# Windowed attention with block summaries and a two-layer MLP in one kernel: new loading order at the start, a private tile for the picking matrix, whole-tile copies at the end, and a newly planned order of all work

## The chip, the cores and the metric

The kernel runs on one core of a Trainium2 chip. The metric is the device time of one execution in microseconds (us), smaller is better. Five engines work side by side, each in its own fixed order: PE (TensorE, matrix products), DVE (VectorE), ACT (ScalarE), POOL (GpSimd) and SP (SyncE, which here issues nearly all DMA transfers). They wait for one another by semaphores.

## The reference, cut to what matters

```python
def _attn_ref(q, k, v):                       # 4 batches, 8 heads, 768 positions, 64 per head
    k_sum = k.reshape(B, H, nb, 32, D).max(axis=3)       # 24 block summaries of the keys
    v_sum = v.reshape(B, H, nb, 32, D).mean(axis=3)      # and of the values
    mask_l = np.abs(pos[:, None] - pos[None, :]) < 16    # near keys only
    ...
    a = softmax(concat([near scores, scores against k_sum + log(32)]))
    return a @ concat([v, v_sum])

def _moe_ref(x, w_in, w_out):                 # x: 3072 x 512 from the attention
    h = x @ w_in                              # 512 -> 2048
    g = h * erf(softplus(h))
    return g @ w_out                          # 2048 -> 512
```

## The kernel before

**Tiling.** The 3072 rows are 6 chunks of 512. A chunk's attention is 4 *quads* (`qd`), each two heads by 512 queries. A block of 64 queries multiplies a window of 96 keys (`LW`) and the 24 summaries (`NS`), 120 columns (`NK`) in all. Quads 0 to 3 of the first batch are special: their keys are cut out of the plain transposed keys (`kfirst`, tiles `kf`) instead of a prepared window array. The first block has 16 keys of zero padding ahead of it, and `near` in `scores` multiplies the first 16 real keys in their stead, for the mask hides those columns. The summaries of the first batch's values come from PE: `vsum_first` multiplies the values (`vt`) by a 0/1 matrix `pick`, in six matmuls to one bank, `vs`. ACT copies the result to `vsum`, and `rows_` spreads it under the value windows `vwf`, which `load_vw_first` had filled with 128 partitions, zeros at the bottom.

**A quad's path.** `scores` (PE, L597), maxima, exponentials and norm (DVE L636, ACT L644, DVE L654; from quad 4 on a fused DVE operation at L630), `transp` (PE L684 and copies to the tile `pt` at L689; from quad 8 on DVE and a trip through DRAM, `dt` out and `ptd` back), `av` (PE L729 or L732, output `px`), `xsplit` (x as a high and a low part, the low one at DVE L748).

**MLP.** The weights come as raw 64-bit numbers (`rw`, L334, 1024 KB a unit). `convert` makes 32-bit floats of them on DVE (L354, L357, L360), and `split` a high part (ACT) and a low part (DVE L376), both in `w`. `mm1` (PE L836) takes three products of the high and low parts, and from period 8 on `products` (L879 to L888) takes fewer products of sums. `mm2` is L1006 (two periods) and L1010, three products of the split tiles `gh` and `gl`; `gl` is made at DVE L993. A period is 512 rows by 512 hidden columns, 24 in all.

**Order.** The code adds each piece of work to a `Plan` with booked times per engine, and `Plan.order` plays the engines against each other and hands out an order for each one. `TUNE` shifts single pieces by number: an offset of the sorting key, a price for changing ACT's function table, which table, and an engine. Where a piece may run on two engines, `order` picks one. At the start `busy` fills expected waits of PE with matmuls on zeros (tile `idle`, L1058). `first_dma` books the first transfers.

**End.** `evac_last` empties the last four banks. For the tiles 0 to 2, ACT copies one half and DVE the other, each to a tile of its own and with a transfer of its own; tile 3 is copied whole by ACT and sent in two halves, from ACT's and SP's queues.

Of the kernel before, what the change touches and what calls it, by code (L numbers as in the profile page):

```python
# [11 lines left out]
F32 = mybir.dt.float32  # L12
# [10 lines left out]
C, F = 512, 2048  # L23
# [168 lines left out]
def block_attention_mlp(ctx: ExitStack, tc: tile.TileContext, q_t, k_nat, k_win, v_tok, v_nat, v_win, w_in, w_out, out):  # L192
# [91 lines left out]

# [9 lines left out]
    def first_dma(us, fn, r=(), w=(), **kw):  # L294
        return P.add({"SP": us}, lambda e: fn(), r, w, hold=2.0, land=-1.0, **kw)
# [216 lines left out]

    def load_v_first():
        for n in range(2):
            first_dma(2.1 + 0.15 * n, lambda n=n: nc.sync.dma_start(out=vts[n], in_=v_tok[3 * n:3 * n + 3].rearrange("t s c -> s t c")), w=[f"vt{n}"])  # L515

    def load_vw_first(p):
        first_dma(1.35, lambda: nc.sync.dma_start(out=st[p]["vw"], in_=v_win[0, p]), w=[f"vwf{p}"])

    def ksum_first(p):  # L520
        on({"DVE": 0.86}, lambda e: e.tensor_reduce(ksum[:, 0, p], groups(kfirst[p]), op=ALU.max, axis=AX.X), [f"kf{p}"], [f"ksum0{p}"])

    def vsum_first(bank):
        def go(t):
            if t == 0:
                tiles[bank] = ps("vs", bank)
            nc.tensor.matmul(tiles[bank][0:NK], lhsT=pick[:, 20 - 4 * t:140 - 4 * t], rhs=vts[t // 3][:, t % 3], start=(t == 0), stop=(t == 5))
        for t in range(6):
            pe(0.87, lambda t=t: go(t), [f"vt{t // 3}"], [bank])
        def summed():  # L530
            nc.scalar.copy(vsum[LW:NK], tiles[bank][LW:NK].rearrange("s (p c) -> s p c", p=NP))
        act(0.5, summed, [bank], [f"vsum0{p}" for p in range(NP)])
        def rows_(e, p):
            o, i = st[p]["vw"][LW:NK], vsum[LW:NK, p:p + 1, :].to_broadcast([NS, NB, 128])
            e.dma_start(out=o, in_=i) if e is nc.sync else copy(e, o, i)
        for p in range(NP):
            on({"ACT": 0.95, "SP": 0.45} if p else {"DVE": 1.13, "ACT": 0.95}, lambda e, p=p: rows_(e, p), [f"vsum0{p}", f"vwf{p}"], [f"vwg{p}"])
# [36 lines left out]

    PA = ("pA", "pB")

    def scores(qd, banks=PA):
# [29 lines left out]
        if qd >= NP:  # L607
            pe(0.98 if qd >= MQ else 1.56, both, [f"qb{qd % 2}", f"kw{qd % 2}"] + (["mh"] if qd < MQ else []), banks, small=1)
        else:
            pe(0.58, mask, ["mh"], banks, small=1)  # L610
            pe(0.96, lambda: keys(near), [f"qf{qd}", f"kf{qd}"], banks, small=1)
            pe(0.5, lambda: keys(lambda r, j: [(LW, ksum[r, 0, qd])]), [f"qf{qd}", f"ksum0{qd}"], banks, small=1)
# [104 lines left out]
    def av(qd, bank):  # L717
# [3 lines left out]
        def go():  # L721
            xo = s["xo"] = ps("px", bank)
            for j in range(NB):
                o = slice(64 * j, 64 * j + 64)
                for a in range(2):
                    r = slice(64 * a, 64 * a + 64)
                    if qd < DT:
                        b = 64 * (NI * a + j // 2)
                        nc.tensor.matmul(xo[r, o], lhsT=s["vw"][0:NK, j, r], rhs=s["pt"][0:NK, j % 2, b:b + 64], start=True, stop=True)  # L729
# [586 lines left out]
```

## Time and profile before

| what | value |
|---|---|
| median of 3 runs | 601.16 us (600.86 to 601.78) |
| the profiled execution: its span | 599.2 us, 2.0 us under the median of the runs, which also hold what lies around the span |
| PE busy | 591.9 us, 99% |
| DVE, ACT busy | 476.3 us (79%), 425.4 us (71%) |
| function tables loaded by ACT in the loop | 98, 125.7 us |
| DMA | 169.94 MB, 284 GB/s on average |

The profiled execution is given by its span alone; the runs' times are the larger number. In every row of the trace below times are from the start of that span. A matmul of PE overlaps the next one: what counts is the distance from one start to the next, not the length of a row.

### The profile page before, as it was taken

Reading aid. Unit: us, or ns where it says so; the run is one execution under the profiler, and the core shown is the slowest. Engines: PE = TensorE matmul, PEld = TensorE weight load, DVE = VectorE, ACT = ScalarE, POOL = GpSimd, SP = SyncE. Lnnn points to the kernel's source line nnn. Section 1 sums busy time; section 2 is a strip of 40 time slices with the busy share of each in tenths; the row PEclk is TensorE's granted clock in tenths of the full one; section 3 lists DMA queues with packets and bytes.
Section 4 is the critical chain, followed back from the end, with each engine's and each line's share of the span. In section 5 each row is a group of like instructions: output and inputs, shape, how many; then the busy total and the mean of one; then the engine's idle time right before and its main releaser. Section 6 shows DMA issues by size and latency. Waiting matters only on the chain.

```text
span 599.2 us, 11732 instructions
## 1 busy us (share of the span) xinstructions
PE 591.9 (99%) x4515; PEld 486.9 (81%) x4515; DVE 476.3 (79%) x1001; ACT 425.4 (71%) x827; POOL 4.0 (1%) x30
## 2 busy tenths in 40 slices
PE   8999999999999999999999999999999999999997
PEld 4675666878888889889888888888888888888885
DVE  5999999888999987867989769669778677656552
ACT  6989889989979894674886964746646654852571
POOL 2000000000000000000000000000000000000000
PEclk9999999999999999999999999999999999999999
DMA  8999768578987989899898889777798863764622
GB/s 313 350 412 357 288 232 308 205 258 293 314 349 244 363 310 336 307 357 363 311 366 315 321 315 326 284 278 284 261 320 275 298 236 141 259 236 175 244 71 71
DMA packets 47955, 169.94 MB, mean 284 GB/s; under 512 B 4444, under 2 KB 17692, under 8 KB 35356
## 3 DMA queue, kind: packets, MB, share of 16 engines
q1 hardware_dynamic: 47324, 168.67, 77.7%
q8 instruction: 35, 0.57, 0.4%
q10 hardware_dynamic: 576, 0.52, 0.3%
q14 instruction: 20, 0.16, 0.1%
HBM read 135.66 MB, written 31.46 MB: 279 GB/s over the span
## 4 chain that ended last, share of the span: by engine, by line
PE 95%; DMA 2%; DVE 1%; SPq 1%; issue 0%; ACT 0%; DVEq 0%
PE ops L1010 41%; PE h L836 15%; PE ha L888 11%; PE hb L882 7%; PE ops L1006 5%; PE hb L888 4%; PE hb L879 4%; PE pA L597 3%; PE px L732 3%; DMA rw<-w_in 2%; PE px L729 1%; PE pA L684 1%; PE pB L597 0%; SPq L515 0%; SPq L511 0%; SPq L510 0%
## 5 line engine op out<-in xcount | busy, mean ns | idle before, releaser
L1010 PE MATMUL ops<-w,gh 128*128 128x512 f32 x704 | 230.2, 393 | 0.0
L1010 PEld LDWEIGHTS ops<-w,gh 128*128 128x128 f32 x704 | 132.3, 188 | 27.7 <-issue 0.9
L1010 PE MATMUL ops<-w,gl 128*128 128x512 f32 x352 | 137.5, 391 | 0.0
L1272 ACT ACT_TABLE_LOAD x98 | 125.7, 1283 | 1.7
L836 PE MATMUL h<-x,w 128*128 128x512 f32 x384 | 97.1, 402 | 0.0
L298 ACT COPY hc<-hb 128x256 f32<-128x256 f32 x65 | 23.9, 373 | 102.0 <-PE hb L879 55.9
L836 PEld LDWEIGHTS h<-x,w 128*128 128x128 f32 x384 | 71.1, 188 | 18.5 <-issue 3.7
L1010 PEld LDWEIGHTS ops<-w,gl 128*128 128x128 f32 x352 | 66.2, 188 | 11.8
L986 DVE TENSOR_TENSOR hc<-wt,hc 128x1024 f32<-128x1024 f32 x44 | 53.0, 1219 | 10.7 <-ACT wt L974 10.7
L644 ACT ACTIVATE prx<-prx,stats 128x120 f32<-128x120 f32 x160 | 61.0, 384 | 0.2
L993 DVE TENSOR_TENSOR gl<-hc,gh 128x1024 fp32r<-128x1024 f32 x44 | 53.6, 1220 | 1.0 <-ACT gh L298 0.2
L927 DVE TENSOR_TENSOR hc<-hb,hc 128x256 f32<-128x256 f32 x96 | 38.7, 418 | 15.8 <-ACT hc L298 14.8
L974 ACT ACTIVATE wt<-wt 128x1024 f32<-128x1024 f32 x48 | 50.1, 1059 | 0.4
L962 ACT ACTIVATE wt<-hc 128x1024 f32<-128x1024 f32 x32 | 33.0, 1056 | 8.2 <-DVE hc L927 8.0
L298 DVE CAST gh<-hc 128x1024 fp32r<-128x1024 f32 x37 | 25.5, 690 | 10.6 <-PE ops L1010 9.5
L882 PE MATMUL hb<-w,ws 128*128 128x512 f32 x96 | 30.2, 396 | 0.0
L644 ACT ACTIVATION_READ_ACCUMULATOR prx<-prx,stats 128x1 f32 x160 | 30.0, 188 | 0.0
L1006 PE MATMUL ops<-a32s,gw 128*128 128x512 f32 x64 | 29.6, 597 | 0.0
L630 DVE CUSTOM_DVE_ANT_0 prx<-pA,mask_sb 128x120 f32<-128x120 f32 x64 | 14.2, 278 | 17.7 <-PE pB L597 17.5
L298 DVE COPY hc<-hb 128x256 f32<-128x256 f32 x31 | 13.0, 418 | 18.0 <-PE hb L879 13.9
L888 PE MATMUL ha<-w,ws 128*128 128x256 f32 x192 | 27.2, 283 | 0.0
L888 PE MATMUL ha<-x,w 128*128 128x256 f32 x192 | 27.2, 282 | 0.0
(173 smaller groups left out, 961.8 us busy)
## 6 DMA issues: line engine op xcount, KB each, us to landing
w<-dr SPq DMA_DIRECT2D x36, 1024.0 KB
ws<-ds SPq DMA_DIRECT2D x30, 1024.0 KB
vw<-v_win SPq DMA_DIRECT2D x20, 512.0 KB
kw<-k_win SPq DMA_DIRECT2D x20, 480.0 KB
rw<-w_in SPq DMA_DIRECT2D x8, 1024.0 KB
rw<-w_out SPq DMA_DIRECT2D x8, 1024.0 KB
dr<-w SPq DMA_DIRECT2D x8, 1024.0 KB
dt<-ot SPq DMA_DIRECT2D x16, 512.0 KB
```

The source lines that it names most:

```text
L298: e.copy(o, i) if e is nc.scalar else e.tensor_copy(o, i)
L644: nc.scalar.activation(s["pr"][:, j], s["pr"][:, j] if qd >= MQ else s["sc"][j // NI][:, i * NK:(i + 1) * NK], AF.Exp, scale=-1.0 if qd >= ...
L836: nc.tensor.matmul(hs[k, f][:, 0:T], lhsT=w[m], rhs=xt[ch, cc][:, x], start=(cc == 0 and n == 0), stop=(cc == 3 and n == 2))
L882: nc.tensor.matmul(full, lhsT=w[0], rhs=y, start=first and c == 0, stop=c == 1, skip_group_check=True)
L888: nc.tensor.matmul(half, lhsT=w[m], rhs=y[:, l], start=first and c == 0 and i == 0, stop=c == 1 and i == 2, skip_group_check=True)
L927: on({"DVE": 0.43}, lambda e: e.tensor_tensor(hc[k, n][:, m, z], bank(n, "b")[:, R], hc[k, n][:, m, z], op=ALU.add), [pair_banks(n)[1]], [ ...
L974: act(0.96, lambda n=n: nc.scalar.activation(wt[k, n], wt[k, n], AF.Erf, scale=-1.0 if k < SOFT else 1.0), [s], [s], table=("sig",), after ...
L986: e.tensor_tensor(hc[k, n], wt.pop((k, n)), hc[k, n], op=ALU.mult)
L993: e.tensor_tensor(gs[k, n][1], hc.pop((k, n)), f32(gs[k, n][0]), op=ALU.subtract)
L1006: nc.tensor.matmul(os_[ch, t], lhsT=x[0][:, i % 2, t * 128:(t + 1) * 128], rhs=w32["o", g, i // 2][:, i % 2], start=first, stop=last)
L1010: nc.tensor.matmul(os_[ch, t], lhsT=x[y][:, i % 2, t * 128:(t + 1) * 128], rhs=w[m], start=first and n == 0, stop=last and n == 2)
L1272: nc.scalar.preload_act_table_set(sets[o["load"]])
```

## The change

Seven edits: `near` leaves the 16 stand-in columns out (two matmuls a quad, eight in all). `load_qk_first` adds the queries' transfer ahead of the keys', and its bookings change, as do those of the other first transfers. `pick` has a tile of its own and no longer the place of `pt`. `load_vw_first` loads 96 partitions and not 128, so that it no longer overlaps the rows that `rows_` writes; those may now go by SP, ACT or DVE. `evac_last` copies every tile whole, tiles 0 to 2 on DVE with one transfer each. `busy` is asked for fewer matmuls for the same expected wait. `TUNE` is a new table of 1244 entries in place of 1111, with 4 entries the same. Code for `OWN` and `ASKED` comes in too, but both are empty, and it does nothing.

```diff
-TUNE = {3: (-38.72167, 1.5, 0, None), 4: (-0.388519, 1.5, 0, None),
...
+TUNE = {3: (0.2407978, 1.5, 0, None), 10: (-0.1088595, 1.5, 0, None),
...
-    pick = sb([128, 140], F32, "pick", "pt")
+    pick = sb([128, 140], F32, "pick")
...
-        return P.add({"SP": us}, lambda e: fn(), r, w, hold=2.0, land=-1.0, **kw)
+        return P.add({"SP": us}, lambda e: fn(), r, w, hold=2.0, land=-0.9, **kw)
...
-            first_dma(2.6, go, w=[f"w{n}"])
+            first_dma(2.5, go, w=[f"w{n}"])
...
-        first_dma(2.7 if p == 1 else 0.97, lambda: nc.sync.dma_start(out=kfirst[p], in_=k_nat[0, p]), w=[f"kf{p}"])
         first_dma(0.66, lambda: nc.sync.dma_start(out=qfs[:, p], in_=q_t[0, p]), w=[f"qf{p}"])
+        first_dma(0.97 if p else 0.9, lambda: nc.sync.dma_start(out=kfirst[p], in_=k_nat[0, p]), w=[f"kf{p}"])
...
-        first_dma(1.35, lambda: nc.sync.dma_start(out=st[p]["vw"], in_=v_win[0, p]), w=[f"vwf{p}"])
+        first_dma(0.98, lambda: nc.sync.dma_start(out=st[p]["vw"][0:LW], in_=v_win[0, p, 0:LW]), w=[f"vwf{p}"])
...
-        act(0.5, summed, [bank], [f"vsum0{p}" for p in range(NP)])
+        on({"ACT": 0.55, "DVE": 0.6}, lambda e: copy(e, vsum[LW:NK], tiles[bank][LW:NK].rearrange("s (p c) -> s p c", p=NP)), [bank], [f"vsum0{p}" for p in range(NP)])
...
-            return [(0, kn[r, k0:k0 + LW])] if j else [(0, kn[r, 0:16]), (16, kn[r, 0:LW - 16])]
+            return [(0, kn[r, k0:k0 + LW])] if j else [(16, kn[r, 0:LW - 16])]
...
-        on({"ACT": 0.4}, lambda e: go(e, 0), [f"o{t}"], [f"xl{t}", f"xh{t}"])
-        on({"DVE": 0.4}, lambda e: go(e, 1), [f"o{t}"], [LAST[t]])
+        def whole(e):
+            ob = sb([128, C], F32, "ob", f"x{t}")
+            copy(e, ob, os_[NCH - 1, t])
+            for n, q in enumerate((nc.scalar, nc.sync) if t == NT - 1 else (nc.sync,)):
+                c = slice(n * 256, n * 256 + 256) if t == NT - 1 else slice(0, C)
+                q.dma_start(out=out[r:r + 128, c], in_=ob[:, c])
+        on({"ACT": 0.59} if t == NT - 1 else {"DVE": 0.69}, whole, [f"o{t}"], [f"xl{t}", f"xh{t}"])
...
-                busy(int(max(0.0, o["start"] - last) / 0.31))
+                busy(int(max(0.0, o["start"] - last - 0.1) / 0.43))
```

What the new plan does to the order is seen at three places. First the transfers that SP issues at the start, before and then after. In both, the rows are for quads in the order of their addresses: before, the first row is quad 1's queries (`qf`), and then come quad 0's keys (`kf`), quad 0's queries and quad 1's keys.

```order
L511 DMA qf<-q_t 128x512
L510 DMA kf<-k_nat 128x768
L511 DMA qf<-q_t 128x512
L510 DMA kf<-k_nat 128x768
L515 DMA vt<-v_tok 128x3x512
L510 DMA kf<-k_nat 128x768
L511 DMA qf<-q_t 128x512
L515 DMA vt<-v_tok 128x3x512
L334 DMA rw<-w_in 128x2048
```

After, quad 0's keys and queries are the first two rows (the lines of the two calls have changed places):

```order
L511 DMA kf<-k_nat 128x768
L510 DMA qf<-q_t 128x512
L511 DMA kf<-k_nat 128x768
L510 DMA qf<-q_t 128x512
L515 DMA vt<-v_tok 128x3x512
L511 DMA kf<-k_nat 128x768
L510 DMA qf<-q_t 128x512
L515 DMA vt<-v_tok 128x3x512
L334 DMA rw<-w_in 128x2048
```

The four transfers ahead of the first `vt` have changed places among themselves; the same nine stand ahead of and at the first unit of weights (`rw`).

Second, what DVE does from the first unit of weights on, before: `a_348` becomes the first 32-bit weights, `ksum` is quad 3's key summaries, `prf` is a quad's probabilities (quad 2's here), `stats<-h` are quad 3's maxima.

```order
L354 TENSOR_SCALAR a_348<-rw 128x1024
L357 SCALAR_TENSOR_TENSOR a_348<-rw,a_348 128x1024
L521 TENSOR_REDUCE ksum<-kf 128x24
L360 SCALAR_TENSOR_TENSOR a_348<-rw,a_348 128x1024
L648 TENSOR_SCALAR stats<-stats 128x8
L649 RECIPROCAL stats<-stats 128x8
L636 TENSOR_REDUCE stats<-h_312 128x4
L636 TENSOR_REDUCE stats<-h_313 128x4
L638 TENSOR_SCALAR stats<-stats 128x8
L376 TENSOR_TENSOR w<-a_348,w 128x1024
L654 TENSOR_TENSOR prf<-prf,stats 128x960
L748 TENSOR_TENSOR x<-px,x 128x512
```

After, the same stretch without its first row (L354 on `a_339`, which stands ahead of it as before), up to the low part of the first weights; `a_441<-rw` is the first step of the second unit of weights, which before follows the twelve rows above:

```order
L357 SCALAR_TENSOR_TENSOR a_339<-rw,a_339 128x1024
L521 TENSOR_REDUCE ksum<-kf 128x24
L653 TENSOR_SCALAR stats<-stats 128x8
L654 RECIPROCAL stats<-stats 128x8
L360 SCALAR_TENSOR_TENSOR a_339<-rw,a_339 128x1024
L659 TENSOR_TENSOR prf<-prf,stats 128x960
L641 TENSOR_REDUCE stats<-h_342 128x4
L641 TENSOR_REDUCE stats<-h_343 128x4
L643 TENSOR_SCALAR stats<-stats 128x8
L758 TENSOR_TENSOR x<-px,x 128x512
L354 TENSOR_SCALAR a_441<-rw 128x1024
L376 TENSOR_TENSOR w<-a_339,w 128x1024
```

Quad 2's norm (L654, then L659) and quad 0's low part of x (L748, then L758) have moved ahead of the low part of the first weights (L376).

Third, DVE's last six rows, before and after, where `ops` with a number is one of the last four banks:

```order
L986 TENSOR_TENSOR hc_6025<-wt_6112,hc_6025 128x1024
L298 CAST gh_6149<-hc_6025 128x1024
L993 TENSOR_TENSOR gl_6150<-hc_6025,gh_6149 128x1024
L298 COPY ob_6183<-ops_5748 128x256
L298 COPY ob_6195<-ops_5729 128x256
L298 COPY ob_6214<-ops_5753 128x256
```

```order
L996 TENSOR_TENSOR hc_5996<-wt_6095,hc_5996 128x1024
L298 CAST gh_6135<-hc_5996 128x1024
L1003 TENSOR_TENSOR gl_6136<-hc_5996,gh_6135 128x1024
L298 COPY ob_6160<-ops_5702 128x512
L298 COPY ob_6169<-ops_5750 128x512
L298 COPY ob_6178<-ops_5707 128x512
```

The halves have become whole tiles. Before, PE's last matmul is for the bank of DVE's last copy (`ops_5753`, one of the tiles 0 to 2, whose other half ACT copies); after, it is for tile 3's bank, which ACT copies whole.

## Rows read from the trace of the kernel before

**Rows 1.** The page: busy time of each engine in us (share of the span, instructions).

```profile
PE 591.9 (99%) x4515; PEld 486.9 (81%) x4515; DVE 476.3 (79%) x1001; ACT 425.4 (71%) x827; POOL 4.0 (1%) x30
```

**Rows 2.** Stretches: length, busy us by engine, granted clock (PEclk), DMA share, GB/s.

```profile
4.00:8.00 4.00, 3.37 (x96) 2.36 (x98) 1.92 (x4) 1.80 (x3) 1.22 (x12) 1.00 0.92 281
8.00:17.00 9.00, 8.13 (x163) 4.83 (x155) 7.97 (x16) 7.10 (x41) 0.00 (x0) 1.00 1.04 410
26.00:105.00 79.00, 79.00 (x563) 52.61 (x560) 78.59 (x135) 71.01 (x143) 0.00 (x0) 1.00 0.85 316
```

**Rows 3.** Order of time, PE: start, length, line, tiles, count [idle before].

```profile
1.06 3.03 PE L1058 MATMUL idle<-zeros 128*128 128x512 bf16 x7 [1.06 <-DVE zeros L217]
...
22.95 1.68 PE L1058 MATMUL idle<-zeros 128*128 128x512 bf16 x7
25.36 0.24 PE L684 MATMUL pA<-ident,prf 64*120 64x64 f32 x1 [0.72 <-DVE prf L654]
...
27.28 3.72 PE L836 MATMUL h<-x,w 128*128 128x512 f32 x15
```

**Rows 4.** Order of time, DVE, from the first unit of weights on.

```profile
17.26 0.69 DVE L354 TENSOR_SCALAR a<-rw 128x1024 uint32<-128x1024 uint32 x1 [0.24 <-DMA rw<-w_in]
...
24.06 1.15 DVE L654 TENSOR_TENSOR prf<-prf,stats 128x960 f32<-128x960 f32 x1
25.13 0.68 DVE L748 TENSOR_TENSOR x<-px,x 128x512 fp32r<-128x512 f32 x1
...
26.46 1.23 DVE L357 SCALAR_TENSOR_TENSOR a<-rw,a 128x1024 uint32<-128x1024 uint32 x1
```

**Rows 5.** Order of time, DVE and PE, around the first split product.

```profile
103.82 1.21 DVE L993 TENSOR_TENSOR gl<-hc,gh 128x1024 fp32r<-128x1024 f32 x1
...
105.98 0.39 PE L1010 MATMUL ops<-w,gl 128*128 128x512 f32 x1
...
106.21 0.39 PE L1010 MATMUL ops<-w,gh 128*128 128x512 f32 x1
```

**Rows 6.** DVE's groups until 106 us, by shape: count, busy us, mean ns.

```profile
L376 DVE TENSOR_TENSOR w<-a,w 128x1024 fp32r<-128x1024 f32 x11 | 13.4, 1217 | 0.0
...
L474 DVE TENSOR_REDUCE ksum<-rows 128x24 f32<-128x768 f32 x5 | 4.7, 936 | 0.0
...
L298 DVE COPY kw<-ksum 128x96 f32<-128x96 f32 x3 | 0.6, 202 | 0.0
```

**Rows 7.** Order of time, PE, around one island of scores.

```profile
142.09 0.39 PE L1010 MATMUL ops<-w,gh 128*128 128x512 f32 x1
142.41 0.31 PE L597 MATMUL pA<-kw,qb 64*64 64x120 f32 x1
...
143.39 0.50 PE L1010 MATMUL ops<-w,gh 128*128 128x512 f32 x1
143.73 0.40 PE L1010 MATMUL ops<-w,gl 128*128 128x512 f32 x1
```

**Rows 8.** Order of time, all engines and queues, at the end.

```profile
594.72 0.59 ACT L1042 COPY ob<-ops 128x512 f32<-128x512 f32 x1 [1.21 <-PE ops L1010]
...
594.98 0.39 PE L1010 MATMUL ops<-w,gh 128*128 128x512 f32 x1
...
595.34 0.36 ACTq L1045 DMA_DIRECT2D out<-ob  x1
595.40 0.42 DVE L298 COPY ob<-ops 128x256 f32<-128x256 f32 x1 [2.29 <-PE ops L1010]
...
596.26 0.34 ACTq L1038 DMA_DIRECT2D out<-ob  x1
```

**Rows 9.** Order of time, SP's queue, and PE, at one of the late quads.

```profile
252.64 0.37 SPq L705 DMA_DIRECT2D ptd<-dt  x1
...
261.19 0.63 PE L732 MATMUL px<-ptd,vw 120*64 120x64 f32 x14
```

More of the change, by code (lines that the diff above doesn't have):

```diff
@@ L509, in load_qk_first @@
         st[p] = dict(qb=qfs[:, p], vw=vws[p // 2][:, p % 2])
-        first_dma(2.7 if p == 1 else 0.97, lambda: nc.sync.dma_start(out=kfirst[p], in_=k_nat[0, p]), w=[f"kf{p}"])
         first_dma(0.66, lambda: nc.sync.dma_start(out=qfs[:, p], in_=q_t[0, p]), w=[f"qf{p}"])
+        first_dma(0.97 if p else 0.9, lambda: nc.sync.dma_start(out=kfirst[p], in_=k_nat[0, p]), w=[f"kf{p}"])
     def load_v_first():
         for n in range(2):
-            first_dma(2.1 + 0.15 * n, lambda n=n: nc.sync.dma_start(out=vts[n], in_=v_tok[3 * n:3 * n + 3].rearrange("t s c -> s t c")), w=[f"vt{n}"])
+            first_dma(2.5 + 0.7 * n, lambda n=n: nc.sync.dma_start(out=vts[n], in_=v_tok[3 * n:3 * n + 3].rearrange("t s c -> s t c")), w=[f"vt{n}"])
     def load_vw_first(p):
-        first_dma(1.35, lambda: nc.sync.dma_start(out=st[p]["vw"], in_=v_win[0, p]), w=[f"vwf{p}"])
+        first_dma(0.98, lambda: nc.sync.dma_start(out=st[p]["vw"][0:LW], in_=v_win[0, p, 0:LW]), w=[f"vwf{p}"])
     def ksum_first(p):
@@ L529, in vsum_first, with rows_ @@
             pe(0.87, lambda t=t: go(t), [f"vt{t // 3}"], [bank])
-        def summed():
-            nc.scalar.copy(vsum[LW:NK], tiles[bank][LW:NK].rearrange("s (p c) -> s p c", p=NP))
-        act(0.5, summed, [bank], [f"vsum0{p}" for p in range(NP)])
-        def rows_(e, p):
+        on({"ACT": 0.55, "DVE": 0.6}, lambda e: copy(e, vsum[LW:NK], tiles[bank][LW:NK].rearrange("s (p c) -> s p c", p=NP)), [bank], [f"vsum0{p}" for p in range(NP)])
+        def rows_(e, p, ask=False):
             o, i = st[p]["vw"][LW:NK], vsum[LW:NK, p:p + 1, :].to_broadcast([NS, NB, 128])
-            e.dma_start(out=o, in_=i) if e is nc.sync else copy(e, o, i)
+            e.dma_start(out=o, in_=i) if ask or e is nc.sync else copy(e, o, i)
         for p in range(NP):
-            on({"ACT": 0.95, "SP": 0.45} if p else {"DVE": 1.13, "ACT": 0.95}, lambda e, p=p: rows_(e, p), [f"vsum0{p}", f"vwf{p}"], [f"vwg{p}"])
+            if p in OWN:
+                P.last[f"vwg{p}"] = ()
+            elif p in ASKED:
+                act(0.4, lambda p=p: rows_(nc.scalar, p, True), [f"vsum0{p}", f"vwf{p}"], [f"vwq{p}"])
+                P.add({"POOL": 2.2}, lambda e: None, [f"vwq{p}"], [f"vwg{p}"])
+            else:
+                on({"ACT": 0.95, "SP": 1.0, "DVE": 1.13} if p else {"DVE": 1.13, "ACT": 0.95}, lambda e, p=p: rows_(e, p), [f"vsum0{p}", f"vwf{p}"], [f"vwg{p}"])
     def load_quad(qd):
@@ L575, in block_attention_mlp @@
     PA = ("pA", "pB")
+    OWN, ASKED = (), ()
     def scores(qd, banks=PA):
@@ L610, in scores @@
             pe(0.58, mask, ["mh"], banks, small=1)
-            pe(0.96, lambda: keys(near), [f"qf{qd}", f"kf{qd}"], banks, small=1)
-            pe(0.5, lambda: keys(lambda r, j: [(LW, ksum[r, 0, qd])]), [f"qf{qd}", f"ksum0{qd}"], banks, small=1)
+            pe(0.92, lambda: keys(near), [f"qf{qd}", f"kf{qd}"], banks, small=1)
+            pe(0.57, lambda: keys(lambda r, j: [(LW, ksum[r, 0, qd])]), [f"qf{qd}", f"ksum0{qd}"], banks, small=1)
     def softmax(qd, banks=PA):
@@ L722, in go @@
             xo = s["xo"] = ps("px", bank)
+            for a in range(2 if qd in OWN else 0):
+                r = slice(64 * a, 64 * a + 64)
+                rhs = s["pt"][LW:NK, :, 256 * a:256 * a + 256].rearrange("k x (n q) -> k n x q", n=NI)
+                nc.tensor.matmul(xo[r].rearrange("d (n x q) -> d n x q", n=NI, x=2), lhsT=vsum[LW:NK, qd, r], rhs=rhs, start=True, stop=False, skip_group_check=True)
             for j in range(NB):
@@ L728, in go @@
                         b = 64 * (NI * a + j // 2)
-                        nc.tensor.matmul(xo[r, o], lhsT=s["vw"][0:NK, j, r], rhs=s["pt"][0:NK, j % 2, b:b + 64], start=True, stop=True)
+                        nk = LW if qd in OWN else NK
+                        nc.tensor.matmul(xo[r, o], lhsT=s["vw"][0:nk, j, r], rhs=s["pt"][0:nk, j % 2, b:b + 64], start=qd not in OWN, stop=True, skip_group_check=qd in OWN)
                     else:
@@ L732, in go @@
                         nc.tensor.matmul(xo[r, o].rearrange("d (a q) -> d a q", a=2), lhsT=s["vw"][0:NK, j, r], rhs=s["pt"][0:NK, z:z + 2, NI * a + j // 2], start=True, stop=True)
-        pe(1.085, go, ["pt", "vw"] if qd >= NP else ["pt", f"vwf{qd}", f"vwg{qd}"], [bank], small=1)
+        pe(2.1 if qd in OWN else 1.15 if qd < NP else 1.085, go, ["pt", "vw"] if qd >= NP else ["pt", f"vwf{qd}", f"vsum0{qd}" if qd in OWN else f"vwg{qd}"], [bank], small=1)
     xt = {}
@@ L1027, in evac @@
         dma(262, lambda: nc.sync.dma_start(out=out[ch * T + t * 128:ch * T + (t + 1) * 128], in_=tiles["ob", t]), home)
-    LAST = ("qb0", "kw0", "kw1", "vw")
     def evac_last(t):
         r = (NCH - 1) * T + t * 128
-        def go(e, n):
-            c = slice(n * 256, n * 256 + 256)
-            ob = sb([128, 256], F32, "ob", LAST[t] if n else f"x{t}")
-            copy(e, ob, os_[NCH - 1, t][:, c])
-            (nc.scalar, nc.sync)[n].dma_start(out=out[r:r + 128, c], in_=ob)
-        if t == NT - 1:
-            def whole():
-                ob = sb([128, C], F32, "ob", f"x{t}")
-                nc.scalar.copy(ob, os_[NCH - 1, t])
-                for n, e in enumerate((nc.scalar, nc.sync)):
-                    c = slice(n * 256, n * 256 + 256)
-                    e.dma_start(out=out[r:r + 128, c], in_=ob[:, c])
-            act(0.59, whole, [f"o{t}"], [f"xl{t}", f"xh{t}"])
-            return
-        on({"ACT": 0.4}, lambda e: go(e, 0), [f"o{t}"], [f"xl{t}", f"xh{t}"])
-        on({"DVE": 0.4}, lambda e: go(e, 1), [f"o{t}"], [LAST[t]])
+        def whole(e):
[5 more added lines that the diff above has]
+        on({"ACT": 0.59} if t == NT - 1 else {"DVE": 0.69}, whole, [f"o{t}"], [f"xl{t}", f"xh{t}"])
     banks = [PA, ("h0", "h1"), ("o0", "o1"), ("h0", "h1")]
```

2 lines of the change are left out of this document (1 added, 1 removed).

## The prediction

> **What bounds the kernel now.** I read the page first, then the busy times by stretch, then the order of time of the first 30 us, of the last 5, and of the place where the first split product is handed over. PE is busy 99% of the span, DVE 79%, ACT 71% [rows 1]. Busy is not the same as useful, so the reader should look for waits: the last wait that PE has in the whole trace is the 0.72 us ahead of 25.36 us, for DVE's norm [rows 3]. From the first MLP matmul at 27.28 us on, PE's matmuls follow one another at their own pace. So the time is the moment at which this dense part begins, plus the work in it, plus the end behind PE's last matmul. An edit counts only if it moves one of the three.
>
> A second engine is as full. From 26 to 105 us DVE is busy 78.59 of 79.00 us [rows 2]. It went into this stretch without a pause: from 17.26 us, where it got the first unit of weights, to 26.46 us, 13 instructions stand end to end [rows 4], which shows the first and three near the end. DVE makes the converted weights, x and the products in this stretch, and PE uses them shortly after. The clearest place is the first split product: its low part is begun at 103.82 us and takes 1.21 us, so it is there at 105.03, and PE's first matmul on it starts at 105.98 [rows 5]. That is 0.95 us of cover. PE can't arrive there earlier than DVE allows, however early its own part begins.
>
> **The beginning.** The order on SP swaps four transfers among themselves, but the same nine stand at and ahead of the first unit of weights, with the same bytes. Quad 0's scores can begin earlier, because one transfer of 256 KB no longer stands ahead of them. That speeds the first softmax, but DVE then waits for the weights: it already waited 0.24 us for them at 17.26 [rows 4]. So I leave DVE's 17.26 where it is. The eight stand-in matmuls, the tile of its own for the picking matrix (which lets quad 0's transposes go ahead of the last picks), the earlier first scores and the shorter value loads all lie ahead of or beside this wait: I cost them at nothing. The wait for the weights hides them; were it gone, they could be worth what the weights' arrival is worth, for which I give bounds below.
>
> From 17.26 on DVE has the same 13 instructions in both orders, 9.20 us of start-to-start distance [rows 4], but the low part of the first weights is now last of them and not two thirds through. It is done some 0.08 us after 26.46, the overlap of one instruction's length (1.23) with the distance to the next. The handover from DVE to PE took 0.15 us at 25.36 (the norm ends at 24.06 + 1.15 = 25.21) [rows 3, 4]. So the first MLP matmul moves from 27.28 to about 26.7 us. Of the work moved ahead, quad 2's norm came before PE's transposes, so that these no longer stand in front of the first MLP matmul with a wait.
>
> **The work in the dense part.** The order shows the same matmuls from there to the first split product, with two differences. One filler matmul is gone: fillers of that time take 1.68 / 7 = 0.24 us each [rows 3]. And the small matmuls of attention stand in 8 islands between MLP matmuls and not in 10. An island costs at both edges: the MLP matmul ahead of it keeps 0.32 us (142.09 to 142.41), the first behind it 0.34 (143.39 to 143.73) [rows 7], where 0.23 is the pace (105.98 to 106.21) [rows 5]. That makes 0.09 + 0.11 = 0.2 us an island, 0.4 for two. PE's part from the first MLP matmul to that product shrinks from 105.98 - 27.28 = 78.70 to 78.70 - 0.24 - 0.40 = 78.06 us. If nothing held it, PE would be there at 26.7 + 78.06 = 104.76, 1.2 us earlier than before.
>
> DVE decides whether it may. Up to that low part its order has one weight subtraction more (1.22), one key reduction fewer (0.94), two small key copies fewer (0.20 each) [rows 6], and one copy of x in place of one of h, of one shape, which I set equal. Net: 1.22 - 0.94 - 0.40 = -0.12 us. So the product is there at 105.03 - 0.12 = 104.91, and PE starts on it 0.15 later, at 105.06. **PE is held 0.3 us and keeps 105.98 - 105.06 = 0.92 us.**
>
> Behind this place the order has 23 islands where it had 22 (31 in all, against 32): 0.20 us back. DVE has air there: over the whole span it is busy 79% against 99% until 105 us [rows 1, 2]. ACT loads 88 tables in the loop and no longer 98, which is 10 times 1.28 us (125.7 / 98) off an engine that is not the bound (71%): nothing, unless ACT held PE, and PE waits for it nowhere.
>
> **The end.** Before, DVE copies one half of the last bank at 595.40, ACT the other behind it, and the last transfer is issued at 596.26 [rows 8]. After, PE's last matmul is for tile 3, which ACT copies whole: from 594.72 to the issue at 595.34 that took 0.62 us [rows 8]. Begun at 595.40 it gives an issue at 596.02, **0.24 us earlier**. The whole-tile copies of DVE for the others lie under PE's remaining matmuls; I cost them at nothing. Without that cover one costs its length, which a 128x256 copy of 0.42 bounds from below and twice that from above.
>
> **The unseen cost: when the first weights land.** DMA moved 281 GB/s from 4 to 8 us and 410 from 8 to 17 [rows 2]. If the new order of the first four transfers avoided all of that dip, 4 x (1 - 281/410) = 1.26 us would come off, and DVE's whole chain with it. If the dip is the same or moves, it is nothing, or a few tenths worse. The bytes are the same, so I stay near zero and take 0.1 us, with -0.3 and 1.26 as bounds. Three spreading copies now go by SP and wait there for ACT's sum; behind them stand loads of values and the third and fourth units of weights. I cost this at nothing, since DVE asks for the third unit only behind the 13 instructions named above, more than 9.2 us after the first; late by more than that cover, it would hold DVE one for one.
>
> **Sum.** -0.92 + 0.20 - 0.24 - 0.10 = -1.06 us on a span of 599.2. The runs' median is 601.16, 2.0 above that span, and I leave this part as it is: **600.1 us**, 0.18% less. A measurement of this kernel can tell about 0.2% (1.2 us) from no change, so 599.96 and 602.36 are the borders of "same", and the forecast stands close to the lower one.
>
> **Rivals.**
> *The weights land early, or DVE is not the limit.* For it: DVE's norm of quad 1 can be done about a microsecond before 17.26 now, since the first scores begin earlier, so an early landing would be used; and the dip from 4 to 8 us is there to be lost. Against it: the same bytes. With 0.9 us of the 1.26 the sum is -1.9, 599.3 us.
> *A late return from DRAM (the other side).* From quad 8 on the probabilities go out to DRAM and back ahead of `av`. One of these returns was issued at 252.64, and its matmuls began at 261.19, 8.55 us later [rows 9]. The last transfer of all took 599.2 - 596.26 = 2.9 us, so some 5.6 us is cover. SP's order is new throughout; a load of 1024 KB is 2.6 us at 410 GB/s [rows 2], so three more ahead of a return pass the cover, and from then on PE waits one for one. To end slower than 602.36 PE must lose 3.3 us; I price it at one wait of 3.5 us: 600.1 + 3.5 = 603.6 us. Against it: PE waits for no transfer after 26 us now.
> *The clock.* The first seven fillers took 3.03 / 7 = 0.43 us each and the later seven 0.24 [rows 3]: the two levels, 1.2 and 2.4 GHz; in all stretches shown the granted clock is 1.00, the upper one [rows 2]. The new order has 12 fillers where there were 17, and none ahead of the picks, where PE may stand still more than a microsecond. Should the clock fall there, PE's work of the next stretch, about as long as the 3 us at the start, takes twice the time, partly hidden: up to +1.5 us, 601.6. The Trainium skill, "TensorE: Matmul & The Clock Gate", Part 1, says that the throttled clock is the default and that activity releases it, and its table at the end warns of idle gaps between bursts: by that rule taking fillers out is a risk. The trace has no fall to show.
> *The plan gives nothing.* Some new waits of a few tenths each eat the lead, and only the end is left: 600.9.
>
> **Chances and range.** Forecast (599.6 to 600.8) 0.52, of which 0.14 below 599.96; early weights 0.26; late return 0.10; clock 0.05; nothing 0.07. Faster: 0.14 + 0.26 = 0.40; slower 0.10; same 0.50. The range leaves out the late return and the outer part of the early weights: 599.0 to 601.3. The likeliest case alone is 599.6 to 600.8.
>
> **What would show it.** First MLP matmul at about 26.7 us; DVE's first unit of weights at 17.2; DVE without a pause to about 105 us; the first split matmul near 105.1 with PE waiting for DVE a few tenths on the way; the last issue 0.6 us behind PE's last end. Wrong if the weights' first step on DVE starts well before 17, if PE shows a wait of more than a microsecond behind 105 us, or if fillers' distances are 0.43 again after 10 us.

## The result and the profile after

| | before | after |
|---|---|---|
| median of 6 runs | 601.12 us (600.86 to 601.78) | 605.55 us (603.27 to 606.28) |
| ratio, 95% interval | | 1.0066 [1.0054, 1.0078] |
| profiled execution: time, span | 601.16, 599.2 us | 604.92, 602.7 us |

The change makes the kernel 4.4 us, 0.66%, slower; the forecast was 600.1 us, range 599.0 to 601.3. The runs after also lie further apart: 3.0 us from lowest to highest, 0.9 before.

PE's busy share hardly shows it (98%, 99% in [rows 1]). What shows it is PE's order of time, which answers to [rows 3] (start, length, line, tiles, count, idle time before):

```profile
21.60 0.91 PE L739 MATMUL px<-ptr,vwf 120*64 120x64 f32 x23
25.03 0.77 PE L739 MATMUL px<-ptr,vwf 120*64 120x64 f32 x9 [2.52 <-issue]
25.73 1.89 PE L1057 MATMUL idle<-zeros 128*128 128x512 bf16 x4
...
29.66 3.69 PE L846 MATMUL h<-x,w 128*128 128x512 f32 x15
33.54 1.15 PE L739 MATMUL px<-ptr,vwf 120*64 120x64 f32 x32 [0.19 <-ACT prf L662]
...
38.74 1.15 PE L739 MATMUL px<-ptr,vwf 120*64 120x64 f32 x32 [1.17 <-DVE a L354]
```

The first quad's `av` is 32 matmuls in one piece. PE does 23 of them, stops for 2.52 us, and does the other 9. "Issue" means that the profile shows nothing that PE waited for. Then the four fillers take 1.89 / 4 = 0.47 us each, near the 0.43 of the first seven and not the 0.24 of the later ones in [rows 3]: the lower clock, 1.2 GHz. The first MLP matmul starts at 29.66, where 26.7 was forecast and 27.28 had been. Behind it PE waits again, 0.19 and 1.17 us, ahead of the `av` of quads 2 and 3; before, it waited nowhere there.

The stretches answer to [rows 2]; the row of the kernel before for 17.0 to 22.5 us stands below them. The last three numbers are granted clock, DMA share and GB/s.

```profile
4.00:8.00 4.00, 2.81 (x73) 1.85 (x71) 1.40 (x2) 1.75 (x2) 1.22 (x12) 1.00 0.90 303
8.00:17.00 9.00, 8.63 (x158) 5.22 (x159) 8.00 (x18) 7.09 (x37) 0.00 (x0) 1.00 1.04 392
17.00:22.50 5.50, 4.80 (x111) 3.18 (x109) 5.43 (x9) 4.97 (x17) 0.00 (x0) 1.00 1.04 265
22.50:26.00 3.50, 0.98 (x11) 0.71 (x11) 1.24 (x3) 0.17 (x1) 0.00 (x0) 0.87 1.05 257
26.00:40.00 14.00, 12.64 (x157) 9.39 (x156) 12.60 (x16) 11.40 (x36) 0.00 (x0) 0.91 1.02 320
```

```profile
17.00:22.50 5.50, 5.30 (x114) 3.39 (x111) 5.19 (x9) 4.81 (x14) 0.00 (x0) 1.00 1.03 415
```

From 17.0 to 22.5 us the 16 DMA engines are as full as before (1.04, 1.03), but they move 265 GB/s and not 415. This is the time of the value loads with 96 partitions. And in both stretches behind 22.5 us the granted clock is under 1: asked for more finely, it is 0.50 from 25.1 to 28.5 us, so from the end of the stop on, and 1.00 again from 28.5 to 40.

DVE, answering to [rows 4]:

```profile
17.15 0.69 DVE L354 TENSOR_SCALAR a<-rw 128x1024 uint32<-128x1024 uint32 x1
...
26.45 0.69 DVE L758 TENSOR_TENSOR x<-px,x 128x512 fp32r<-128x512 f32 x1 [2.68 <-ACT x L298]
27.06 0.68 DVE L354 TENSOR_SCALAR a<-rw 128x1024 uint32<-128x1024 uint32 x1
27.66 1.22 DVE L376 TENSOR_TENSOR w<-a,w 128x1024 fp32r<-128x1024 f32 x1
```

DVE gets the first weights at 17.15, as forecast. Then it waits 2.68 us for the first quad's x, which waits for PE's `av`; the low part of the first weights behind it is done at 27.66 + 1.22 = 28.88 us. PE's first MLP matmul is later still, at 29.66, and waits for nothing: it stands right behind PE's own fillers, transposes and `av`, which come after the stop and run at the lower clock until 28.5.

At the first split product ([rows 5]) DVE and PE are 3.6 and 3.3 us later than before, and PE still does not wait for DVE, whose product is there at 108.65:

```profile
107.43 1.22 DVE L1003 TENSOR_TENSOR gl<-hc,gh 128x1024 fp32r<-128x1024 f32 x1
...
109.29 0.40 PE L1020 MATMUL ops<-w,gl 128*128 128x512 f32 x1
```

From there the distance stays: PE's last matmul starts 3.46 us later than in [rows 8].

```profile
598.44 0.39 PE L1020 MATMUL ops<-w,gh 128*128 128x512 f32 x1
598.87 0.58 ACT L298 COPY ob<-ops 128x512 f32<-128x512 f32 x1 [11.31 <-PE ops L1020]
599.48 0.37 ACTq L1047 DMA_DIRECT2D out<-ob  x1
```

So the loss is made between 17 and 40 us. In the traced execution the first MLP matmul is 2.38 us later and the two waits behind it are 1.36; from there to the split product PE's work is 0.43 shorter, which makes the 3.31. Two things in that stretch were costed at nothing, and SP's queue shows how they meet:

```profile
11.10 0.35 SPq L334 DMA_DIRECT2D rw<-w_in  x1
19.94 0.98 SPq L533 DMA_DIRECT2D vwf<-vsum  x1
20.98 0.48 SPq L518 DMA_DIRECT2D vwf<-v_win  x1
21.50 0.43 SPq L334 DMA_DIRECT2D rw<-w_in  x1
21.97 0.83 SPq L533 DMA_DIRECT2D vwf<-vsum  x1
...
24.45 0.82 SPq L533 DMA_DIRECT2D vwf<-vsum  x1
```

SP issues nothing from 11.45 to 19.94 us: it waits for the sum that the first spreading transfer reads, and the third unit of weights behind it is issued at 21.50, where before it was issued at 14.61. The three spreading transfers then stand behind slow loads. By the landing events in the trace, quad 2's is complete at 33.30 us and quad 3's at 38.61; their `av` start at 33.54 and 38.74. The list of waits names ACT and DVE there. The DVE instruction that it names ends at 38.60, next to the landing, but `av` does not need it: in the kernel e1 below, the same `av` starts at 38.10, while the same DVE instruction runs from 37.92 to 38.61.

### The profile page after: what moved, and what is told of

Its sections match the earlier page's. It is cut to its first block, busy times and chain, and to the rows that moved or that the text cites. A ratio compares the mean times of both kernels' runs of the same rounds, so it can differ in the third digit from the quotient of the medians.

```text
span 602.7 us, 11683 instructions
## 1 busy us (share of the span) xinstructions
PE 591.5 (98%) x4494; PEld 486.9 (81%) x4494; DVE 474.5 (79%) x996; ACT 409.4 (68%) x817; POOL 4.0 (1%) x30
## 4 chain that ended last, share of the span: by engine, by line
PE 88%; DVE 5%; DMA 3%; ACT 2%; SPq 1%; issue 0%; DVEq 0%; ACTq 0%
PE ops L1020 40%; PE ha L898 11%; PE h L846 11%; PE hb L892 7%; PE hb L898 4%; PE hb L889 4%; PE px L742 3%; PE pA L602 3%; PE ops L1016 2%; DMA rw<-w_in 2%; DMA qf<-q_t 1%; PE vs L527 1%; PE px L739 1%; ACT L1271 1%; DVE a L360 1%; DVE a L357 1%
## 5 line engine op out<-in xcount | busy, mean ns | idle before, releaser
L1020 PE MATMUL ops<-w,gh 128*128 128x512 f32 x704 | 227.2, 392 | 0.0
L298 ACT COPY hc<-hb 128x256 f32<-128x256 f32 x69 | 25.4, 372 | 126.0 <-PE hb L889 74.4
L846 PE MATMUL h<-x,w 128*128 128x512 f32 x384 | 93.3, 397 | 0.0
L898 PE MATMUL ha<-x,ws 128*128 128x256 f32 x192 | 26.9, 283 | 0.0
```

Source lines behind the costliest of these rows:

```text
L298: e.copy(o, i) if e is nc.scalar else e.tensor_copy(o, i)
L846: nc.tensor.matmul(hs[k, f][:, 0:T], lhsT=w[m], rhs=xt[ch, cc][:, x], start=(cc == 0 and n == 0), stop=(cc == 3 and n == 2))
L898: nc.tensor.matmul(half, lhsT=w[m], rhs=y[:, l], start=first and c == 0 and i == 0, stop=c == 1 and i == 2, skip_group_check=True)
L1020: nc.tensor.matmul(os_[ch, t], lhsT=x[y][:, i % 2, t * 128:(t + 1) * 128], rhs=w[m], start=first and n == 0, stop=last and n == 2)
```

## The experiments

**What the stop is.** The page of the kernel after counts one transfer of instructions for some 257 instructions of PE, (4494 + 4494) / 35:

```profile
PE 591.5 (98%) x4494; PEld 486.9 (81%) x4494; DVE 474.5 (79%) x996; ACT 409.4 (68%) x817; POOL 4.0 (1%) x30
...
q8 instruction: 35, 0.57, 0.4%
```

Between 15.0 and 22.4 us no such block is moved, and at the stop's beginning (25.03 - 2.52 = 22.51) one is. The transfers of the two stretches:

```profile
DMA packets 544, 2.07 MB, mean 280 GB/s; under 512 B 65, under 2 KB 65, under 8 KB 440
...
q1 hardware_dynamic: 544, 2.07, 104.0%
```

```profile
DMA packets 22, 0.08 MB, mean 397 GB/s; under 512 B 3, under 2 KB 14, under 8 KB 14
...
q1 hardware_dynamic: 21, 0.06, 84.5%
q8 instruction: 1, 0.02, 34.1%
```

The block starts at 22.47 and PE goes on at 25.03, 2.56 us later. The Trainium skill, "Runtime: NRT & Kernel Launch", Instruction fetch mechanics, says that instructions come in blocks of 256 over a queue of their own while the engine works on the current one. The trace agrees with the size. The page also says that this is mostly hidden; here 2.52 us of it are not. Theory A2 in the expectations below is this: a block is asked for when PE passes into the one ahead of it, so 256 records ahead of the stop, which is in the first quad's transposes at 14.9 us; and the block came too late. That the block ahead is what asks for it is the theory's guess; no trace shows the asking.

**Narrow loads or spreading by SP.** The first two kernels change the functions behind the plan, so that the order stays.

```diff
# e1_wide_act: both edits; e2_narrow_act: the second alone
-        ... nc.sync.dma_start(out=st[p]["vw"][0:LW], in_=v_win[0, p, 0:LW])
+        ... nc.sync.dma_start(out=st[p]["vw"], in_=v_win[0, p])
-            e.dma_start(out=o, in_=i) if ask or e is nc.sync else copy(e, o, i)
+            copy(nc.scalar if e is nc.sync else e, o, i)
```

> The changed kernel with two of its edits undone: the four value loads have 128 partitions again, and the three spreading copies that went by SP are copied by ACT at their place in the order. Everything else, PE's and DVE's order too, is that of the changed kernel. Theory A (narrow loads: with 96 partitions the queue moves 265 GB/s between 17.0 and 22.5 us where it moved 415, and what stands behind, PE's next block of instructions first of all, comes late): more than 380 GB/s from 17.0 to 22.5, no stop in the first quad's av, first MLP matmul at 26.7 to 27.4 us, 600.0 to 601.5 us. Theory B (the spreading transfers on SP, and SP's wait for the sum, are the cause): the same times. Theory C (the new order itself loses the time, later or elsewhere): 604 or more.

> The changed kernel with 96-partition loads kept, and only the three spreading copies given to ACT at their place in the order. Theory A: 17.0 to 22.5 us stays below 320 GB/s, a stop of more than 1 us without a named releaser stays in PE's first 30 us, the first MLP matmul is at 28.5 us or later, and only the wait of 1.17 us ahead of quad 3's av goes: 603.3 to 605.0 us. Theory B: no stop, first MLP matmul at 27.4 us at the latest, 600.0 to 601.5 us.

Measured: e1 604.60 us, 1.0060 [1.0048, 1.0072]; e2 607.17 us, 1.0092 [1.0071, 1.0114], above both of its ranges. The stretch and the stop of e1, then of e2:

```profile
17.00:22.50 5.50, 4.22 (x110) 3.01 (x108) 5.43 (x9) 5.36 (x14) 0.00 (x0) 1.00 1.03 416
...
24.07 0.50 PE L739 MATMUL px<-ptr,vwf 120*64 120x64 f32 x9 [2.75 <-issue]
```

```profile
17.00:22.50 5.50, 3.87 (x90) 2.47 (x90) 5.43 (x8) 5.42 (x16) 0.00 (x0) 0.96 1.04 258
22.50:26.00 3.50, 1.41 (x23) 1.22 (x23) 1.08 (x3) 0.21 (x1) 0.00 (x0) 0.50 1.06 276
...
28.07 0.80 PE L739 MATMUL px<-ptr,vwf 120*64 120x64 f32 x9 [4.16 <-issue]
```

With 128 partitions the queue is back at 416 GB/s and the kernel 2.6 us faster than e2. (The traced execution of e2 is the slowest of its six, which go from 603.97 to 608.45.) But the stop stays, so theory A (the slow loads make the block late) and theory B (the spreading) both fall as the cause of it. Theory C, the order, was left.

```diff
# e3_before_narrow: the kernel before, with
-        ... out=st[p]["vw"], in_=v_win[0, p])
+        ... out=st[p]["vw"][0:LW], in_=v_win[0, p, 0:LW])
```

> The kernel before with one edit of the change alone: its four value loads have 96 partitions and not 128, so a quarter fewer bytes; the order is unchanged on every engine. Theory A: less than 330 GB/s somewhere between 17 and 26 us at full DMA share where it was 415, and the time rises to 602 to 605 us, although fewer bytes are moved. Theory B or C: 600.6 to 601.6 us, no difference, or a little faster.

Measured: 602.71 us, 1.0033 [1.0021, 1.0045]. A quarter fewer bytes in four loads, the order untouched, and 1.9 us slower:

```profile
17.00:22.50 5.50, 4.31 (x93) 2.57 (x94) 4.51 (x8) 5.04 (x14) 0.00 (x0) 1.00 1.04 253
...
33.08 1.15 PE L729 MATMUL px<-ptr,vwf 120*64 120x64 f32 x32 [1.51 <-DMA vwf<-vsum]
```

The Trainium skill, "SBUF — State Buffer", "Can I just issue two DMAs to hit both halves?", says that only a transfer over all 128 partitions reaches all 16 ports. The rows agree in direction; for 96 partitions the page has no figure, and no run here shows what held these loads up.

**Is it the count of instructions?** Four kernels shift PE's stream.

```diff
# e4_more_instr: the changed kernel, with
-    busy(WARM)
+    short(WARM + 29)          # matmuls of 64x64 on zeros
```

> The changed kernel with the seven filler matmuls at its start replaced by 36 short ones of 64x64, so that PE has 29 matmuls more ahead of everything; these fillers compute nothing that is used. If the stop of 2.52 us is PE running out of instructions, it stays tied to the count of records: it comes 29 matmuls earlier in the program, and so no longer behind the 23rd matmul of the first av but within the scores against the key summaries of quad 3 or just ahead of that av; the time stays at 604 to 606.5 us. If the stop is a wait of av for data, it stays behind av's 23rd matmul, or at av's first.

Measured: 605.97 us, 1.0074 [1.0051, 1.0096]. The stop did not move, it went: the block starts at 17.6 us. The time is no better, since PE then waits 2.89 us until 28.64 for quad 1's spreading transfer, which lands at 28.51 by its landing events, and the granted clock falls there (0.76 from 26 to 40 us). Neither guess was right, but that the stop depends on the count was the new lead.

```diff
# f1_wide_act_near: e1, f2_near: the changed kernel, each with the stand-ins back
-            ... else [(16, kn[r, 0:LW - 16])]
+            ... else [(0, kn[r, 0:16]), (16, kn[r, 0:LW - 16])]
```

> As e1_wide_act, and the eight stand-in matmuls of the first blocks are back: three edits of the change undone, its order kept. Theory A2 (PE runs out of instructions: they come in blocks of 256, the second block is asked for where the first is used up, and whether it comes in time depends on when PE passes that place; 24 of the records taken out by the edit lay ahead of it, so that without them PE passes it at 14.3 to 14.9 us, behind its wait for the first probabilities, and with them at about 13.3 us): no stop in the first quad's av, block fetched at 17 to 19 us, first MLP matmul at 26.7 to 27.5, time 600.0 to 602.0 us. Rival A3 (the stop depends on the new transfers of SP alone, not on the count of instructions): the stop of 2.5 us or more stays, and the time is 604 to 605 us.

> The changed kernel with the eight stand-in matmuls back and nothing else: loads of 96 partitions and spreading by SP stay. Theory A2: no stop that is put down to issue, but PE still waits for the spreading transfers ahead of av, 1 to 3 us in all, since these stand behind the slow loads: 602 to 605 us. Rival A3: the stop of 2.5 us stays, 604.5 to 606.5 us.

Measured: f1 603.16 us, 1.0035 [1.0022, 1.0048]; f2 605.35 us, 1.0066 [1.0051, 1.0080], a little above the range of A2. In both the stop in `av` is gone. Both have a short one earlier (1.09 us in f1, 0.85 in f2, ahead of 14.10 and 14.25 us), at the place where PE passes into the block before. The kernel before has that one too:

```profile
13.74 0.31 PE L597 MATMUL o<-ksum,qf 64*64 64x24 f32 x7 [0.55 <-issue]
```

In f1 the next block comes within this stretch,

```profile
DMA packets 114, 0.42 MB, mean 422 GB/s; under 512 B 11, under 2 KB 11, under 8 KB 113
...
q8 instruction: 1, 0.02, 6.5%
```

17 to 18 us, and the first MLP matmul is at 26.95. f1 is 1.4 us faster than e1, but above its range: PE now waits 0.99 us at 24.77 and 1.52 at 37.15 for copies of ACT, which has three spreading copies more. In f2 a wait of 2.96 us ahead of quad 1's `av` takes the place of the stop; its spreading transfer lands at 28.42 us, and that `av` starts at 28.56.

```diff
# h1_wide_act_24 and h2_wide_act_8: e1, with
-    busy(WARM)
+    busy(5); short(14)        # h2: busy(6); short(5)
```

> As e1_wide_act, with two of the seven fillers at the start replaced by 14 short ones of 64x64: 12 matmuls, 24 records more ahead of everything, as many as the stand-ins of three quads, and no stand-ins. If the count of instructions decides: no stop in the first av, block fetched at 17 to 19.5 us, first MLP matmul at 26.5 to 27.5, 602 to 604 us like f1_wide_act_near. If it was the stand-ins themselves (what they do to the time of the scores): the stop of 2.5 us stays, 604 to 605.2 us.

> As e1_wide_act, with one filler replaced by 5 short ones: 4 matmuls, 8 records more. The place where the block is used up still lies in the transposes of the first quad. If what matters is that this place is passed inside these transposes, behind their wait: the stop stays, behind about the 19th matmul of the first av and no longer behind the 23rd, 604 to 605.2 us. If any shift is enough: no stop, 602 to 604 us.

Measured: h1 603.01 us, 1.0033 [1.0021, 1.0045], no stop in `av`; h2 602.91 us, 1.0030 [1.0018, 1.0041]. PE in h2:

```profile
20.72 0.80 PE L739 MATMUL px<-ptr,vwf 120*64 120x64 f32 x19 [0.16 <-ACT vwf L298]
22.43 0.77 PE L739 MATMUL px<-ptr,vwf 120*64 120x64 f32 x13 [0.91 <-issue]
```

Four matmuls more at the start, and the stop stands behind the 19th and not the 23rd. That is the count, shown. Counting PE's records (matmuls and weight loads) in all 18 traces says the same: every stop of 0.25 us or more that is put down to issue in the first 45 us, 13 in all, stands behind exactly 449 records (eight kernels, the one before among them) or 706 (five), 257 apart, and PE goes on 2.4 to 2.7 us after the start of a block's transfer each time. The stop in h2 is shorter than expected, and the time as if there were none: of its six executions the traced one alone has a granted clock under 0.999 (0.996). h1 has no stand-ins and, with no stop in `av`, behaves like f1: it is not they, but their 24 records.

**What spreading costs elsewhere, and the single parts in the old order.**

```diff
# f4_wide_sp_near: f1, with
-            copy(nc.scalar if e is nc.sync else e, o, i)
+            e.dma_start(out=o, in_=i) if ask or e is nc.sync else copy(e, o, i)
# g4_before_sp: the kernel before, with
-            e.dma_start(out=o, in_=i) if e is nc.sync else copy(e, o, i)
+            nc.sync.dma_start(out=o, in_=i) if p else copy(e, o, i)
```

> As f1_wide_act_near, but the three spreading copies go by SP as in the changed kernel; since loads of 128 partitions write the same rows, SP then waits for each load to land ahead of its spreading transfer. It tells what the spreading by SP costs when the loads are fast and the instructions come in time: as costed in the prediction nothing, so the time of f1_wide_act_near within 0.6 us; if the transfers behind them come late or av waits for them, 1 to 4 us more than f1_wide_act_near, with a wait for vwf ahead of the av of quads 1 to 3.

> The kernel before with the three spreading copies of quads 1 to 3 all by SP (before, quad 3's alone is); loads keep 128 partitions. As costed in the prediction, nothing: 600.6 to 601.7 us, since the transfers queued behind still find a full queue. If spreading by SP itself costs, by SP's wait for ACT's sum or by a late landing ahead of av: 602 to 604 us, with waits of PE for vwf.

Measured: f4 603.26 us, 1.0034 [1.0022, 1.0047], the time of f1, with other waits: 0.56 and 1.65 us ahead of the `av` of quads 2 and 3. So f4 fits both ends of its expectation and settles little. g4 is clear: 602.70 us, 1.0030 [1.0018, 1.0042], and the list names the transfer:

```profile
38.01 1.15 PE L729 MATMUL px<-ptr,vwf 120*64 120x64 f32 x32 [1.40 <-DMA vwf<-vsum]
```

```diff
# f3_before_no_near: the kernel before without the stand-ins
# g1_before_parts: f3, with evac_last of the change
# g3_quad0_first: the kernel before, SP's first four transfers issued as kf, qf of quad 0, kf, qf of quad 1
```

> The kernel before with this one edit of the change: the eight stand-in matmuls are left out (the mask hides those columns), the order is the same on every engine. As costed in the prediction: nothing, 600.6 to 601.3 us. Theory A2: PE passes the place where it asks for the next block 24 records later, at about 15.5 us and no longer at 13.7, and the block comes at 20 to 24 us, so that PE stops up to 3 us at 22 us; some of it is covered by the fillers and the wait that stood there: 600.6 to 604 us. A stop put down to issue near 22 us would show it.

> The kernel before with two edits of the change: the stand-in matmuls are left out and the last tiles are copied whole; its order, its loads and its spreading copies stay. The prediction's term for the end, -0.24 us, on top of f3_before_no_near (600.48) gives 600.2 us; by the spans of the runs so far, in which the last matmul is followed by 4.15 to 4.27 us of end in both forms, the copies are worth nothing: 600.5 us. Both are faster than the kernel before by 0.1%.

> The kernel before with the new order of the first four transfers alone: keys and queries of quad 0, then those of quad 1. As costed in the prediction, nothing, since DVE waits for the weights behind: DVE's first unit at 17.0 to 17.4 us and 600.5 to 601.6 us. If the dip of the transfers from 4 to 8 us can be lost in this way: DVE's first unit up to 1.26 us earlier and as much off the time. If quad 1, which now comes later, holds DVE's reductions: up to 1 us slower.

Measured: f3 600.48 us, 0.9990 [0.9982, 0.9999]; g1 600.35 us, 0.9995 [0.9985, 1.0005]; g3 601.44 us, 1.0010 [1.0002, 1.0019]. All three are within 0.2%: in the old order these edits cost and bring nothing that counts. f3 also has PE pass the place later, at 15.5 us, without a stop: the block starts at 17.5.

**The new order with all of it mended.**

```diff
# g2_best_new: f4, with
-            e.dma_start(out=o, in_=i) if ask or e is nc.sync else copy(e, o, i)
+            if e is nc.sync and p == 2:
+                held.append(lambda: nc.sync.dma_start(out=o, in_=i))   # issued by the load of quad 3's values
+            elif e is nc.sync and p == 3:
+                e.dma_start(out=o, in_=i)
+            else:
+                copy(nc.scalar if e is nc.sync else e, o, i)
# h3_best_no_near: g2 without the stand-ins;  h4_best_24: h3 with busy(5); short(14)
```

> The new order with loads of 128 partitions and the stand-in matmuls, as f4_wide_sp_near, and the spreading copies where nothing should wait for them: quad 1's by ACT, quad 2's by SP behind the load of quad 3's values, quad 3's by SP where it was. If what is left of the loss (0.7 us in the span of f4_wide_sp_near, 2.3 in f1_wide_act_near) is only waits for spreading copies: first MLP matmul at 25.7 to 27.0 us, waits of PE between 26 and 45 us under 1 us in all, 599.5 to 601.5 us. If the new order loses the time by itself: 602 to 604 us.

> As g2_best_new, but with the stand-in matmuls left out as the change does. If the count of instructions is the cause, PE's stream is that of the changed kernel again, and the stop of 2.5 to 4 us behind the 23rd matmul of the first av comes back although loads and spreading copies are mended: 602 to 605 us. If not: 600.0 to 601.3 us, a little faster than g2_best_new.

> As h3_best_no_near with the fillers of h1_wide_act_24, 24 records more: if the count is the cause, no stop, and the new order without the stand-ins comes to 599.8 to 601.3 us, the time of g2_best_new or a few tenths less; if not, the same as h3_best_no_near.

Measured: g2 601.01 us, 1.0004 [0.9995, 1.0012]; h3 601.27 us, 1.0011 [1.0000, 1.0022]; h4 601.14 us, 1.0004 [0.9995, 1.0013]. The order by itself loses nothing, so theory C falls too. It gains nothing either: with the three losses mended, g2 and h4 take the time of the kernel before and not the 600.1 us of the forecast. h3 has the changed kernel's PE stream, and the stop is back in its old place, with nothing else late:

```profile
20.33 0.91 PE L750 MATMUL px<-ptr,vwf 120*64 120x64 f32 x23
23.88 0.79 PE L750 MATMUL px<-ptr,vwf 120*64 120x64 f32 x9 [2.64 <-issue]
24.60 1.89 PE L1068 MATMUL idle<-zeros 128*128 128x512 bf16 x4
```

Not every execution has it, as far as the granted clock tells, for one of them was traced: of the 11 of h3, six have a mean granted clock of 0.999 or more and take 600.2 to 601.3 us, five have 0.997 or less and take 602.2 to 603.7, as the profiled one (0.997). So the stop came as guessed, but h3's median stays under the 602 to 605 us that went with it. All 11 of h4 have 0.999 or more. Of the six executions of the changed kernel itself one has 0.999, and it is the fastest, 603.27 us; the other five have 0.997 or less and take 604.92 to 606.28.

The first split product in h4:

```profile
103.41 1.22 DVE L1014 TENSOR_TENSOR gl<-hc,gh 128x1024 fp32r<-128x1024 f32 x1
...
105.17 0.40 PE L1031 MATMUL ops<-w,gl 128*128 128x512 f32 x1
```

## Why the prediction was wrong

**The step that failed** is "The beginning": the stand-in matmuls and "the shorter value loads all lie ahead of or beside this wait: I cost them at nothing", and of the spreading copies by SP "I cost this at nothing". The bytes were counted, and not what a transfer of 96 partitions does to the queue, nor what else has to be moved at that time: PE's next instructions.

- *Shorter value loads.* Costed at nothing; alone in the old order +1.9 us (e3), in the new one 2.6 (e2 against e1, both with the stop) and 2.1 (f2 against f4, both without it). The cover that was named, DVE's wait for the first weights, ends at 17.15 us; the loads run behind it.
- *Spreading by SP.* The prediction looked at what is queued behind on SP (the third unit of weights) and not at who waits for the copies themselves. Alone +1.7 us (g4). DVE did wait for that unit and the next, but little: 0.48 us ahead of 32.75 and 0.21 ahead of 37.91.
- *Stand-ins left out.* The work was rightly costed at nothing (f3). But their 24 records shifted PE's stream, and the block of instructions came late: 1.4 us (f1 against e1) to 1.9 (the means of h3's two groups, 602.7 and 600.8). No rival had this.
- *DVE's 17.26 stays*: right in number, 17.15, but partly by luck, since it was not the weights that DVE waited for. By its landing events the first unit is there at 16.33 us and not 17.16, but DVE's norm ends only at 17.23: the early landing (the rival at 599.3) came and was not used.
- *First MLP matmul at 26.7*: 29.66. With the supply mended 25.74 to 26.99 (f4, h4, h1, f1, g2), around the forecast. But f3 and g1, in which PE's order is the same, have 26.77 and 27.79, so a single trace can't tell a gain of 0.6 us.
- *Lead of 0.92 us kept, split product at 105.06*: 109.29; in h4 105.17, but not in the way that was forecast: there the first MLP matmul starts at 26.27, PE then loses 0.55 us in waits for ACT, and DVE holds it nowhere, for its product is there at 103.41 + 1.22 = 104.63. Nor is the lead in the time. From the first MLP matmul to the last matmul of all, less PE's waits, it is 567.3 to 568.2 us in the ten traces of the new order with a granted clock of 1.00 there, and 567.7 to 568.3 in the six of the old: the work in the dense part did not shrink, and the step "DVE decides whether it may" was wrong as well.
- *The end, -0.24*: from the last matmul's start to the last issue 1.04 us and not 1.28, as forecast; but to the end of the span it is 4.2 us in both: what was issued earlier landed no earlier. Over all traces it is 4.05 to 4.23 with whole tiles and 4.10 to 4.23 with halves, so next to nothing is there in other executions either.
- *The clock.* Told as a rival with 0.05, with the condition "PE may stand still more than a microsecond". It stood 2.52 us, and the clock fell; so it came as a follower of the stop and not by the fillers. The late return from DRAM did not come: behind 45 us no wait of PE is in the list.

The parts taken alone in the old order, +1.9, +1.7 and -0.6 (f3), and 1.4 to 1.9 for the stop, give 4.4 to 4.9 us; 4.4 were measured. That they add up so well is partly luck, since the waits overlap. The better proof is h4: with the loads, the spreading and the count mended together, the new order is back at the time of the kernel before.

**Open:** why the block comes so late. From PE's passing of the place to the start of the block it took 7.6, 7.3, 10.8, 7.4 and 6.0 us in the profiled executions of the changed kernel, e1, e2, h3 and h2, where the place lies in the first quad's transposes; in the thirteen others, where it lies elsewhere, it took 2.1 to 5.0, with the DMA engines as full or nearly so. How the queue of instructions gets its turn was not settled.

## What to carry to other kernels

A transfer that moves fewer bytes over fewer partitions can be the slower one: compare GB/s at equal DMA share, and ask what else stands in that queue. Work that costs nothing can still place something: when instructions are added or removed at a time when the DMA engines are full, look for stops put down to "issue", and try whether they move with the count. For a copy that is handed to a queue, look for its consumer, not only for what waits behind it.

## What the hardware showed that was not expected

- 96-partition loads: 242 to 265 GB/s from 17.0 to 22.5 us at a DMA share of 1.03 to 1.04 (the changed kernel, e2, e3, e4, f2), against 415 to 420 at the same share in the eleven kernels whose loads have 128 partitions and whose queue is as full.
- PE goes on some 2.5 us after the start of the transfer that brings its next instructions (22.47 to 25.03, in h3 21.4 to 23.88), and a block's transfer can start 10.8 us after PE has passed into the block ahead of it (e2).
- After a stop of 2.5 us PE came back at the lower clock, 1.2 GHz: fillers at 0.47 us a piece, and 0.50 granted from 25.1 to 28.5 us.
